# Moving the weight preparation of a fused attention and MoE kernel between VectorE and GpSimd

## The chip, the cores and the metric

The kernel runs on one core of one Trainium2 chip. The core has five queues that run side by side and wait for each other by semaphores: TensorE (PE, with its weight loads PEld), VectorE (DVE), ScalarE (ACT), GpSimd (POOL) and SyncE (SP), which here issues all transfers between the chip's main memory and the on-chip buffers. Each queue is strictly in order: an instruction that waits holds up everything behind it on its engine. The metric is the device time of one execution in microseconds (us).

## The reference

Windowed attention over 8 batches, 8 heads, 576 positions and 64 values per head, and behind it a feed-forward layer whose activation is h times softmax(h), normalized and scaled:

```python
scores = scale * np.matmul(q, k.transpose(0, 1, 3, 2))
mask = (rel >= 0) & (rel < window)            # rel = query - key, window = 64
scores = np.where(mask, scores, -1000000000.0)
attn = softmax(scores)                        # maximum taken off, sum + 1e-09
x = (attn @ v)                                # 4608 tokens x 512
h = x @ w_in                                  # 512 x 1024, float64
solu = h * softmax(h)
ln = (solu - mu) / np.sqrt(var + 1e-06) * g_ln
return (ln @ w_out).astype(np.float32)        # 1024 x 512, float64
```

The weights w_in and w_out come as 64-bit floats, which the kernel turns into 32-bit floats itself; g_ln, q, k and v are 32-bit.

## The kernel before

The 4608 tokens are 36 tiles of 128. For each tile t the kernel computes eight heads of scores on TensorE (`scores`, L376, into pS), a softmax (`softmax`), the transposes of the attention weights (`transposes`, L471, copied to PT), the product with v (`values`, L495, into pX, copied to xH and its rest xL), the first feed-forward product (`moe_in`, into pH), the activation and normalization (`moe_norm`, e and the small column buffer mst), a transpose of e, and the second product (`moe_out`, into pO), which is copied out.

A product in full precision is made of three passes with weights split into an upper part H and a rest, here called the lower half (L532, L660). Tiles 0 to 2 in `moe_in` and tile 0 in `moe_out` instead use the whole 32-bit weights in slower plain matmuls (L521, L650), because the split weights are not ready by then.

The weights are prepared during the first tiles. They are eight blocks of 128 x 1024: blocks 0 to 3 are w_in, 4 to 7 are w_out. `weight_block` takes the two 32-bit halves of each 64-bit number: absolute value of the high half (ScalarE, L290), clamp of it to the exponent range (L292), then on VectorE a mask and shift (L294) and two merges with the raw data (L296, L298); for w_out two multiplies by the gain (L302, GpSimd), one for each half of the block. `split` makes the H part (ScalarE, L316) and the lower half as W - H (VectorE, L318), in two halves x = 0 and x = 1 of 512 columns. Lower half i lies in buffer w_(8+i). The ring of w buffers holds nine, so lower half i (i over 0) reuses the buffer of weight block i - 1 and waits for the plain matmuls that read that block.

Softmax: for tile 0 each head has its own instruction on VectorE that adds the mask and takes the minimum of the negated scores (L389), its exponential (ScalarE, L403) and its scale by 1/sum (VectorE, L417). Every other tile has one instruction for all heads' scores (L394) and one for all maxima (L399), and its eight scales are on GpSimd (L417). Tiles 1 to 34 turn e by the transfer engine: `planes` separates the two 16-bit halves of e (VectorE, L592, two instructions a tile, into pl), `turn` stores them (yd) and reads them back transposed (yT). The other tiles turn e on TensorE. The masked attention windows need a joined copy of v (`join`, vx, GpSimd for the first eight tiles). GpSimd also takes the power of the variance (L565) and applies the normalization to e (L569).

The instructions of all queues are recorded as operations with an engine and an estimated cost. `Plan.order` fixes the order of each queue from these costs: it derives from TensorE's recorded order when each operation is due, and places on each engine, among the operations that are ready, the one due first. TensorE's own operations keep the order they were recorded in. A change of an operation's engine or cost so moves others on the same engine. The reads and writes of each operation and the ring sizes give the waits.

Of the kernel before, what the change touches and what calls it, by code (L numbers as in the profile page):

```python
# [36 lines left out]
JOINS = 8  # L37

# [133 lines left out]
def tile_window_attention_solu_moe(  # L172
# [96 lines left out]
    def weight_block(i, src, g):  # L269
# [21 lines left out]
        engine, eng, cost = ("DVE", nc.vector, 700) if i < 2 else ("POOL", nc.gpsimd, 1540)  # L291
        plan.op(engine, cost, lambda: eng.tensor_scalar(  # L292
# [7 lines left out]
        if g is not None:  # L300
            for x in range(2):
                plan.op("POOL", 780, lambda x=x: nc.gpsimd.tensor_scalar(  # L302
                    tf()[:, x], tf()[:, x], g(x), 0.0, ALU.mult, ALU.add), [("g",), W], [("w", i, x)])
# [9 lines left out]
    def split(i):  # L313

        for x in range(2):
            plan.op("ACT", 600, lambda x=x: nc.scalar.copy(WH(i, x), W32(i)[:, x]),  # L316
                    [("w", i), ("w", i, x), ("w", NC + 1 if i < NC else NW - 1)], [("H", i, x)])
            plan.op("DVE", 690, lambda x=x: nc.vector.tensor_sub(  # L318
                WL(i)[:, x], W32(i)[:, x], WH(i, x).bitcast(F32)),
                [("w", i), ("w", i, x), ("H", i, x)], [("w", NW + i, x)])  # L320
# [24 lines left out]
    def join(t):  # L345

        b = t if first_of(t) == 0 else t - 1
        engine, copy, cost = ("POOL", nc.gpsimd.tensor_copy, 780) if t < JOINS else ("ACT", nc.scalar.copy, 590)
        plan.op(engine, cost, lambda: copy(VX(t)[:WIN], V(t)[:WIN]), [("v", t)], [("vx", t, 0)])
        plan.op(engine, cost, lambda: copy(VX(t)[WIN:], V(b)[WIN:]), [("v", b)], [("vx", t, 1)])  # L350

    def SS(t):
        return T("sS", t, [P, H, P])
# [28 lines left out]
    def softmax(t):  # L382
        def cols(tag, h):
            return T(tag, t, [P, H], pool=st)[:, h:h + 1]

        mk = masks[first_of(t)]
        if t == 0:
# [14 lines left out]
        for h in range(H):  # L402
            plan.op("ACT", 580, lambda h=h: nc.scalar.activation(  # L403
                SS(t)[:, h], SS(t)[:, h], AF.Exp, bias=cols("nmx", h), scale=1.0 if t else -1.0,
                accum_out=cols("sm", h)),
                [("nmx", t, h)], [("sS", t, h), ("sm", t, h)], lat=200)
# [8 lines left out]
        engine, v, cost = ("POOL", nc.gpsimd, 400) if t else ("DVE", nc.vector, 150)  # L415
# [170 lines left out]
    def planes(t):  # L586
        if not crosses(t):
            return
        for h in range(2):
            hs = slice(h * 512, (h + 1) * 512)  # L590
            engine, eng, cost = ("DVE", nc.vector, 700)
# [195 lines left out]
```

## Time and profile before

| | us |
|---|---|
| median of 3 runs (lowest to highest) | 562.27 (562.09 to 562.64) |
| profiled execution | 562.74 |
| its span, first to last instruction | 561.0 |
| busy in the span: TensorE | 522.4 (93%) |
| VectorE | 392.4 (70%) |
| ScalarE | 329.9 (59%) |
| GpSimd | 307.8 (55%) |

Busy time is an average over stages. The views used below are the 40 slices of the page (each digit is a tenth of busy time or of full TensorE clock), stretches of time with each engine's busy time, groups of instructions by line and shape, the timeline of one engine, and the chain of work that ended last: followed back from the last instruction, at each step to what released it. In a timeline row the bracket gives the idle time before the instruction and what ended it.

### The profile page before, as it was taken

How to read it: one execution, taken by the hardware profiler on the slowest of the kernel's cores; microseconds unless marked ns; L12 is line 12 of the kernel's file. 1: busy time of each engine (PE TensorE's matmuls, PEld its weight loads, DVE VectorE, ACT ScalarE, POOL GpSimd, SP SyncE). 2: the span in 40 equal slices, each digit the busy share in tenths (PEclk: the TensorE clock that was granted, in tenths of full speed). 3: DMA queues.
4: the chain of work that ended last, by engine and by line, in shares of the span. 5: the costliest groups of instructions: out<-in, count | busy, mean ns of one | idle time of the engine just before them, and what ended most of it. 6: DMA issues, size and time to landing. Idle time of an engine off the chain costs nothing.

```text
span 561.0 us, 11235 instructions
## 1 busy us (share of the span) xinstructions
PE 522.4 (93%) x4088; PEld 401.9 (72%) x4088; DVE 392.4 (70%) x707; ACT 329.9 (59%) x955; POOL 307.8 (55%) x495
## 2 busy tenths in 40 slices
PE   1678679899999999999999999999999999999997
PEld 1334347678788887777777777777777777777865
DVE  4974787767778786868686868676777777755330
ACT  4357565657666666666666666666666677643431
POOL 3839993746556465555555554646464648652110
PEclk9975788999999999999999999999999999999999
DMA  8970211583998999898988998999998995876210
GB/s 350 404 268 20 65 67 43 178 221 123 278 245 234 259 235 236 235 255 221 253 250 238 237 263 235 238 258 232 260 247 227 262 222 177 217 184 164 61 39 37
DMA packets 153079, 115.56 MB, mean 206 GB/s; under 512 B 129856, under 2 KB 129856, under 8 KB 152512
## 3 DMA queue, kind: packets, MB, share of 16 engines
q1 hardware_dynamic: 153024, 114.84, 74.5%
q8 instruction: 32, 0.52, 0.4%
q14 instruction: 23, 0.19, 0.1%
HBM read 41.42 MB, written 41.42 MB: 148 GB/s over the span
## 4 chain that ended last, share of the span: by engine, by line
PE 81%; POOL 6%; DVE 6%; DMA 3%; issue 2%; ACT 0%; SPq 0%; POOLq 0%; ACTq 0%
PE pO L660 36%; PE pH L532 33%; PE pX L495 6%; PE pS L376 6%; POOL sS L417 3%; DMA raw<-w_in 2%; DMA g_sb<-gT 2%; POOL w L292 2%; DVE w L298 1%; DVE sS L394 1%; DVE w L296 1%; DVE mst L547 1%; POOL w L302 1%; DVE w L318 1%; PE t L471 1%
## 5 line engine op out<-in xcount | busy, mean ns | idle before, releaser
L417 POOL TENSOR_SCALAR sS<-sS,rec 128x128 f32<-128x128 f32 x280 | 120.4, 452 | 125.4 <-DVE mst L556 61.8
L403 ACT ACTIVATE sS<-sS,nmx 128x128 f32<-128x128 f32 x288 | 112.0, 392 | 47.1 <-DVE nmx L399 39.9
L660 PE MATMUL pO<-w_outH,yH 128*128 128x512 f32 x280 | 114.7, 410 | 1.6 <-ACT ot L667 1.0
L660 PE MATMUL pO<-w,yH 128*128 128x512 f32 x280 | 110.9, 396 | 0.0
L660 PE MATMUL pO<-w_outH,yL 128*128 128x512 f32 x280 | 110.2, 394 | 0.0
L532 PE MATMUL pH<-w_inH,xH 128*128 128x512 f32 x264 | 106.8, 405 | 1.5 <-DVE mst L552 1.5
L532 PE MATMUL pH<-w,xH 128*128 128x512 f32 x264 | 105.0, 402 | 0.0
L532 PE MATMUL pH<-w_inH,xL 128*128 128x512 f32 x264 | 104.6, 396 | 0.0
L628 DVE TENSOR_TENSOR yL<-yT,yH 128x512 fp32r<-128x512 f32 x66 | 72.0, 1094 | 41.8 <-ACT yH L626 41.7
L569 POOL TENSOR_SCALAR e<-e,mst 128x512 f32<-128x512 f32 x72 | 64.8, 907 | 40.6 <-DVE mst L566 33.3
L626 ACT CAST yH<-yT 128x512 fp32r<-128x512 f32 x66 | 41.0, 622 | 56.6 <-issue 43.8
L547 DVE TENSOR_REDUCE mst<-pH 128x1 f32<-128x1024 f32 x36 | 44.0, 1223 | 38.6 <-PE pH L532 38.3
L660 PEld LDWEIGHTS pO<-w_outH,yH 128*128 128x128 f32 x280 | 52.5, 187 | 19.0 <-issue 4.8
L660 PEld LDWEIGHTS pO<-w_outH,yL 128*128 128x128 f32 x280 | 52.6, 188 | 13.8 <-DVE yL L640 0.9
L532 PEld LDWEIGHTS pH<-w_inH,xH 128*128 128x128 f32 x264 | 50.0, 189 | 14.7 <-ACT w_outH L316 1.6
L660 PEld LDWEIGHTS pO<-w,yH 128*128 128x128 f32 x280 | 52.6, 188 | 10.8
L532 PEld LDWEIGHTS pH<-w_inH,xL 128*128 128x128 f32 x264 | 50.2, 190 | 12.7 <-DVE xL L506 0.3
L532 PEld LDWEIGHTS pH<-w,xH 128*128 128x128 f32 x264 | 50.2, 190 | 11.6 <-issue 0.2
L437 POOL COPY raw<-sS 128x1024 uint16<-128x1024 uint16 x56 | 57.1, 1049 | 0.0
L403 ACT ACTIVATION_READ_ACCUMULATOR sS<-sS,nmx 128x1 f32 x288 | 54.6, 190 | 0.0
L505 ACT CAST xH<-pX 128x512 fp32r<-128x512 f32 x33 | 19.4, 586 | 57.7 <-PE pX L495 57.6
L376 PE MATMUL pS<-qk 64*64 64x128 f32 x1152 | 42.4, 288 | 9.4 <-DMA qk<-qk 7.2
(81 smaller groups left out, 810.4 us busy)
## 6 DMA issues: line engine op xcount, KB each, us to landing
qk<-qk SPq DMA_DIRECT2D x36, 640.0 KB, 4.9
yd<-pl SPq DMA_DIRECT2D x33, 512.0 KB, 3.4
pd<-raw SPq DMA_DIRECT2D x28, 512.0 KB, 3.3
v<-vS SPq DMA_DIRECT2D x36, 256.0 KB, 3.5
y<-ot SPq DMA_DIRECT2D x36, 256.0 KB, 2.6
raw<-w_in SPq DMA_DIRECT2D x4, 1024.0 KB, 9.0
raw<-w_out SPq DMA_DIRECT2D x4, 1024.0 KB, 8.4
yT<-yd SPq DMA_TRANSPOSE x33, 4.9
```

The source lines that it names most:

```text
L376: nc.tensor.matmul(PS(t)[half * WIN:(half + 1) * WIN, r, p], q[rs, p, half * WIN:(half + 1) * WIN], keys, start=True, stop=True)
L403: plan.op("ACT", 580, lambda h=h: nc.scalar.activation(SS(t)[:, h], SS(t)[:, h], AF.Exp, bias=cols("nmx", h), scale=1.0 if t else -1.0, ac ...
L417: plan.op(engine, cost, lambda h=h: v.tensor_scalar(SS(t)[:, h], SS(t)[:, h], rec()[:, h:h + 1], 0.0, ALU.mult, ALU.add), [("rec", t)], [( ...
L437: plan.op(engine, cost, lambda x=x, copy=copy: copy(PP(t)[:, :, 4 * x:4 * x + 4].rearrange("p k h n -> p k (h n)"), SS(t)[:, 4 * x:4 * x + ...
L495: nc.tensor.matmul(PX(t)[r * D:(r + 1) * D, p, ks], (V if half else VX)(t)[:, h * D:(h + 1) * D], PT(t)[:, r * NPAIR + p, ks], start=True, ...
L505: plan.op("ACT", 560, lambda: nc.scalar.copy(XH(t), PX(t)), [("pX", t)], [("xH", t)])
L532: plan.op("PE", 233, lambda n=n, c=c, x=x, w=w: nc.tensor.matmul(PH(t)[:, hs], x(t)[:, c], WH(c, h) if w is WH else WL(c)[:, h], start=(n ...
L547: plan.op("DVE", 1230, lambda: nc.vector.tensor_reduce(nmax(), PH(t), axis=AX.X, op=ALU.max, negate=True), [("pH", t)], [key(0)])
L569: plan.op("POOL", 770, lambda h=h, hs=hs: nc.gpsimd.tensor_scalar(E(t)[:, hs], E(t)[:, hs], nmean(), kk(), ALU.add, ALU.mult), [key(4), ke ...
L626: plan.op("ACT", 560, lambda hs=hs: nc.scalar.copy(YH(t)[:, hs], YT(t)[:, hs]), [("yT", t)], [("yH", t, h)])
L628: plan.op("DVE", 690, lambda hs=hs: nc.vector.tensor_sub(YL(t)[:, hs], YT(t)[:, hs], YH(t)[:, hs].bitcast(F32)), [("yT", t), ("yH", t, h)] ...
L660: plan.op("PE", 233, lambda f=f, i=i, x=x, k=k, y=y, w=w: nc.tensor.matmul(PO(), y(t)[:, f], w(i, x), start=(f == k == 0), stop=(f == NF - ...
```

## The change

Six edits, all in the first tiles' work:

- The clamps of weight blocks 2 to 7 go from GpSimd to VectorE, which had those of blocks 0 and 1.
- The x = 1 half of each lower half goes from VectorE to GpSimd, eight subtractions.
- The planes of the tiles below 4 go from VectorE to GpSimd. Tile 0 has none, so these are tiles 1, 2 and 3.
- Tiles 1 and 2 get their scores and maxima head by head, as tile 0 had.
- The scales of tiles 1 and 2 go from GpSimd to VectorE.
- The estimated costs of some GpSimd operations, and of VectorE's scale, are changed, which only acts on the order.

```diff
+PLANES = 4
+HEADS = 3
+SCALES = 3
...
-        engine, eng, cost = ("DVE", nc.vector, 700) if i < 2 else ("POOL", nc.gpsimd, 1540)
-        plan.op(engine, cost, lambda: eng.tensor_scalar(
+        plan.op("DVE", 700, lambda: nc.vector.tensor_scalar(
             tf(), tf(), EXP_LO, EXP_HI, ALU.max, ALU.min), [W], [W])
...
-                plan.op("POOL", 780, lambda x=x: nc.gpsimd.tensor_scalar(
+                plan.op("POOL", 860, lambda x=x: nc.gpsimd.tensor_scalar(
                     tf()[:, x], tf()[:, x], g(x), 0.0, ALU.mult, ALU.add), [("g",), W], [("w", i, x)])
...
-            plan.op("DVE", 690, lambda x=x: nc.vector.tensor_sub(
+            engine, eng, cost = (("DVE", nc.vector, 690), ("POOL", nc.gpsimd, 1000))[x]
+            plan.op(engine, cost, lambda x=x, eng=eng: eng.tensor_sub(
                 WL(i)[:, x], W32(i)[:, x], WH(i, x).bitcast(F32)),
...
-        engine, copy, cost = ("POOL", nc.gpsimd.tensor_copy, 780) if t < JOINS else ("ACT", nc.scalar.copy, 590)
+        engine, copy, cost = ("POOL", nc.gpsimd.tensor_copy, 860) if t < JOINS else ("ACT", nc.scalar.copy, 590)
...
-        if t == 0:
+        if t < HEADS:
             for h in range(H):
                 plan.op("DVE", 370, lambda h=h: nc.vector.tensor_tensor_reduce(
...
-                SS(t)[:, h], SS(t)[:, h], AF.Exp, bias=cols("nmx", h), scale=1.0 if t else -1.0,
+                SS(t)[:, h], SS(t)[:, h], AF.Exp, bias=cols("nmx", h), scale=-1.0 if t < HEADS else 1.0,
...
-        engine, v, cost = ("POOL", nc.gpsimd, 400) if t else ("DVE", nc.vector, 150)
+        engine, v, cost = ("POOL", nc.gpsimd, 400) if t >= SCALES else ("DVE", nc.vector, 170)
...
-            engine, eng, cost = ("DVE", nc.vector, 700)
+            engine, eng, cost = ("POOL", nc.gpsimd, 1050) if t < PLANES else ("DVE", nc.vector, 700)
             plan.op(engine, cost, lambda h=h, hs=hs, eng=eng: eng.tensor_copy(
                 PL(t)[:, :, hs], E(t)[:, hs].bitcast(U16).rearrange("p (n k) -> p k n", k=2)),
```

Lines behind these edits move by four or five in the changed kernel (L292 becomes L296, L417 becomes L422). TensorE's queue is the same, instruction by instruction. On the other queues the order moves at three places that the prediction speaks of. A name is the buffer's tag, the tile or weight block, and a running number.

VectorE, from the clamp of weight block 1 to the last merge of block 3. Before:

```order
L292 TENSOR_SCALAR w_1_214<-w_1_214 128x1024
L294 TENSOR_SCALAR w_1_214<-w_1_214 128x1024
L296 SCALAR_TENSOR_TENSOR w_1_214<-raw_1_147,w_1_214 128x1024
L294 TENSOR_SCALAR w_2_224<-w_2_224 128x1024
L298 SCALAR_TENSOR_TENSOR w_1_214<-raw_1_147,w_1_214 128x1024
L296 SCALAR_TENSOR_TENSOR w_2_224<-raw_2_149,w_2_224 128x1024
L294 TENSOR_SCALAR w_3_246<-w_3_246 128x1024
L298 SCALAR_TENSOR_TENSOR w_2_224<-raw_2_149,w_2_224 128x1024
L296 SCALAR_TENSOR_TENSOR w_3_246<-raw_3_153,w_3_246 128x1024
L394 SCALAR_TENSOR_TENSOR sS_1_310<-pS_1_252,maskNone_99 128x1024
L298 SCALAR_TENSOR_TENSOR w_3_246<-raw_3_153,w_3_246 128x1024
```

Now, the same stretch:

```order
L296 TENSOR_SCALAR w_1_214<-w_1_214 128x1024
L296 TENSOR_SCALAR w_2_222<-w_2_222 128x1024
L298 TENSOR_SCALAR w_1_214<-w_1_214 128x1024
L298 TENSOR_SCALAR w_2_222<-w_2_222 128x1024
L300 SCALAR_TENSOR_TENSOR w_1_214<-raw_1_147,w_1_214 128x1024
L296 TENSOR_SCALAR w_3_245<-w_3_245 128x1024
L300 SCALAR_TENSOR_TENSOR w_2_222<-raw_2_149,w_2_222 128x1024
L298 TENSOR_SCALAR w_3_245<-w_3_245 128x1024
L302 SCALAR_TENSOR_TENSOR w_1_214<-raw_1_147,w_1_214 128x1024
L300 SCALAR_TENSOR_TENSOR w_3_245<-raw_3_153,w_3_245 128x1024
L302 SCALAR_TENSOR_TENSOR w_2_222<-raw_2_149,w_2_222 128x1024
L302 SCALAR_TENSOR_TENSOR w_3_245<-raw_3_153,w_3_245 128x1024
```

Two clamps have come in, and tile 1's scores stand behind block 3.

GpSimd, from tile 2's join on. Before:

```order
L349 COPY vx_2_293<-v_2_161 64x512
L292 TENSOR_SCALAR w_4_318<-w_4_318 128x1024
L417 TENSOR_SCALAR sS_1_310<-sS_1_310,rec_1_384 128x128 x8
L302 TENSOR_SCALAR w_4_318<-w_4_318,g_sb_110 128x512
L417 TENSOR_SCALAR sS_2_342<-sS_2_342,rec_2_423 128x128 x8
L292 TENSOR_SCALAR w_5_416<-w_5_416 128x1024
L349 COPY vx_3_472<-v_3_163 64x512
L350 COPY vx_3_472<-v_2_161 64x512
L302 TENSOR_SCALAR w_4_318<-w_4_318,g_sb_110 128x512
L292 TENSOR_SCALAR w_6_476<-w_6_476 128x1024
L417 TENSOR_SCALAR sS_3_387<-sS_3_387,rec_3_485 128x128 x8
L292 TENSOR_SCALAR w_7_483<-w_7_483 128x1024
```

Now, the same engine from tile 3's scales on:

```order
L422 TENSOR_SCALAR sS_3_417<-sS_3_417,rec_3_497 128x128 x8
L323 TENSOR_TENSOR w_8_541<-w_0_165,w_inH_108 128x512
L306 TENSOR_SCALAR w_4_317<-w_4_317,g_sb_110 128x512
L354 COPY vx_4_584<-v_4_294 64x512
L355 COPY vx_4_584<-v_3_163 64x512
L306 TENSOR_SCALAR w_4_317<-w_4_317,g_sb_110 128x512
L323 TENSOR_TENSOR w_9_612<-w_1_214,w_inH_108 128x512
L323 TENSOR_TENSOR w_10_620<-w_2_222,w_inH_108 128x512
L422 TENSOR_SCALAR sS_4_548<-sS_4_548,rec_4_618 128x128 x8
L323 TENSOR_TENSOR w_11_673<-w_3_245,w_inH_108 128x512
L306 TENSOR_SCALAR w_6_459<-w_6_459,g_sb_110 128x512 x2
```

The clamps and the scales of tiles 1 and 2 are gone (between tile 2's join and tile 3's scales only tile 3's join and block 5's two multiplies are left), and the subtractions stand among the scales, w_9 to w_11 of which wait for tile 2's plain matmuls.

VectorE at tile 1's scales. Now:

```order
L419 RECIPROCAL rec_1_370<-rec_1_370 128x8
L394 ISA sS_2_353,nmx_2_354<-pS_2_332,maskNone_99 128x128
L394 ISA nmx_2_354 128x1
L422 TENSOR_SCALAR sS_1_311<-sS_1_311,rec_1_370 128x128 x3
L552 TENSOR_REDUCE mst_0_398<-pH_0_297 128x1
L422 TENSOR_SCALAR sS_1_311<-sS_1_311,rec_1_370 128x128 x5
L399 SCALAR_TENSOR_TENSOR sS_3_417<-pS_3_381,maskNone_99 128x1024
L300 SCALAR_TENSOR_TENSOR w_4_317<-raw_4_209,w_4_317 128x1024
L557 ISA e_0_414,mst_0_398<-pH_0_297,e_0_414 128x1024
```

ScalarE, at tile 2's copies, before and now:

```order
L476 COPY PT_2_517<-t_8_504 128x512
L476 COPY PT_2_517<-t_9_511 128x512
L316 CAST w_inH_108<-w_1_214 128x512
L549 ACTIVATE e_1_564,mst_1_519<-pH_1_463,mst_1_519 128x1024
L503 COPY xH_2_571<-pX_2_545 128x512
```

```order
L481 COPY PT_2_538<-t_8_505 128x512
L554 ACTIVATE e_1_543,mst_1_511<-pH_1_462,mst_1_511 128x1024
L481 COPY PT_2_538<-t_9_514 128x512
L320 CAST w_inH_108<-w_1_214 128x512
L320 CAST w_inH_108<-w_2_222 128x512 x2
L508 COPY xH_2_582<-pX_2_557 128x512
```

Five of tile 1's scales stand behind the maximum of pH_0 on VectorE, and on ScalarE tile 1's exponential has moved ahead of tile 2's second copy, three splits now standing ahead of xH_2.

## The prediction

> **What bounds the kernel now.** I read first the page's 40 slices (14 us each), then the engines' busy time by stretch, then the chain of work that ended last.
>
> ```profile
> PE   1678679899999999999999999999999999999997
> PEclk9975788999999999999999999999999999999999
> ```
>
> TensorE fills up only in the eighth slice, and its granted clock dips to half in the fourth. By stretch (us; busy us and instructions of PE, PEld, DVE, ACT, POOL; clock; DMA share; GB/s):
>
> ```profile
> 0.00:114.00 114.00, 80.59 (x649) 50.18 (x649) 84.49 (x143) 61.39 (x174) 80.35 (x108) 0.85 0.50 176
> 38.00:66.00 28.00, 18.92 (x142) 10.45 (x132) 17.38 (x26) 18.96 (x49) 25.51 (x31) 0.73 0.22 66
> 66.00:92.00 26.00, 22.47 (x124) 14.70 (x125) 20.62 (x37) 13.74 (x44) 19.93 (x24) 0.77 0.11 36
> 114.00:500.00 386.00, 386.00 (x3150) 308.43 (x3148) 286.11 (x518) 250.44 (x749) 216.37 (x377) 1.00 0.90 234
> ```
>
> From 114 to 500 TensorE has no gap and a full clock. The change leaves its queue in the same order, so nothing done there by other engines can be worth anything; the gain or loss is how much earlier or later TensorE enters that stretch, with tile 1's first output matmul (pO_1). What sets that moment is in the chain in order of time (start, us, what):
>
> ```profile
> 29.58 2.08 PE pH L521 x2
> ...
> 40.69 3.51 POOL sS L417 x7
> ...
> 44.88 2.83 POOL sS L417 x8
> 47.71 3.59 POOL w L292
> ...
> 59.04 4.81 POOL sS L417 x8
> ...
> 72.12 1.65 DVE w L296
> ...
> 82.23 5.58 PE pH L532 x12
> ...
> 114.01 5.81 PE pO L660 x24
> ```
>
> From 40.7 to 72.1 the chain lies on GpSimd almost without a break, and the row of 38 to 66 has GpSimd busy 25.5 of 28 us: weight clamps (L292), attention scales (L417), gain multiplies. From 72 to 114 it is mostly VectorE. So the start-up is bound by GpSimd, then by VectorE, and TensorE waits.
>
> **The change, part by part.** Durations by group (busy us, mean ns of one; the idle time before follows). All but the copies of L437 and the reduction L547, which are of the whole run, are of the first 116 us:
>
> ```profile
> L292 POOL TENSOR_SCALAR w<-w 128x1024 f32<-128x1024 f32 x6 | 23.2, 3863 | 1.8 <-ACT w L290 1.8
> L292 DVE TENSOR_SCALAR w<-w 128x1024 f32<-128x1024 f32 x2 | 1.4, 688 | 6.7 <-ACT w L290 6.7
> L417 POOL TENSOR_SCALAR sS<-sS,rec 128x128 f32<-128x128 f32 x48 | 22.6, 494 | 13.4 <-DVE rec L414 10.6 <-DVE mst L561 2.8
> L389 DVE CUSTOM_DVE_ANT_0 sS<-pS,mask 128x128 f32<-128x128 f32 x8 | 1.8, 288 | 0.0
> L394 DVE SCALAR_TENSOR_TENSOR sS<-pS,maskNone 128x1024 f32<-128x1024 f32 x7 | 8.5, 1215 | 3.1 <-PE pS L376 3.0
> L318 DVE TENSOR_TENSOR w<-w,w_inH 128x512 fp32r<-128x512 f32 x8 | 6.5, 822 | 0.0
> L592 DVE COPY pl<-e 128x1024 uint16<-128x1024 uint16 x4 | 3.1, 793 | 1.2 <-POOL e L569 1.2
> L437 POOL COPY raw<-sS 128x1024 uint16<-128x1024 uint16 x56 | 57.1, 1049 | 0.0
> L547 DVE TENSOR_REDUCE mst<-pH 128x1 f32<-128x1024 f32 x36 | 44.0, 1223 | 38.6 <-PE pH L532 38.3
> ```
>
> Off GpSimd: six clamps, 23.2 us, and the scales of tiles 1 and 2, 16 x 0.494 = 7.9. Onto it: eight lower halves L318 and the planes of tiles 1 to 3 (tile 0 is turned on TensorE, so "four" is three), six copies. The planes have the shape of L437: 6 x 1.05 = 6.3 us. A two-input 128x512 subtraction on GpSimd is not in the trace. Below, it cannot beat VectorE's 0.82; above, the 128x1024 clamp at 3.86 gives 1.93 for half the columns. I take 1.25, nearer the lower end, because the clamp applies two limits to each element: 8 x 1.25 = 10. GpSimd before 114 goes from 80.4 to 80.4 - 23.2 - 7.9 + 10 + 6.3 = 65.6 us.
>
> The Trainium skill, "GPSIMD Engine Reference", section 4.1 Engine selection, advises against this half of the change: two-input elementwise work belongs on VectorE, being about twice as slow on GpSimd. Its 4497 ns for 2048 columns would make an estimated 1.12 us per subtraction and 9 us for eight. No run here shows it, and the total on GpSimd moves by 1 us.
>
> VectorE gains six clamps (4.1 us) and 16 scales, loses eight subtractions (6.6) and six copies (4.8), and in two tiles trades L394 and an equally long maximum (2.4) for eight heads at 0.29 (2.3). Nothing shows a scale alone on VectorE: tile 0's eight took 2.95 us beside GpSimd's copies (below), 0.37 each; from below 0.21, the step between heads of L389. At 0.3 they cost 4.8. VectorE goes from 84.5 to about 82 us: it does not get lighter, it stops waiting.
>
> **Step 1, tile 0's last weight.** VectorE's timeline (start, us, line, shapes, idle before):
>
> ```profile
> 13.73 2.95 DVE L417 TENSOR_SCALAR sS<-sS,rec 128x128 f32<-128x128 f32 x8
> 16.60 0.68 DVE L292 TENSOR_SCALAR w<-w 128x1024 f32<-128x1024 f32 x1
> 28.15 1.37 DVE L298 SCALAR_TENSOR_TENSOR w<-raw,w 128x1024 int32<-128x1024 int32 x1
> ```
>
> Between 16.60 and 29.52 stand ten weight operations, stretched by GpSimd's clamps, and tile 1's scores. Now twelve weight operations stand there alone: six of 0.69 and six of 1.22 make 11.5; begun 0.8 earlier, since the scales of tile 0 no longer run beside a clamp, they end at 27.3, 2.2 sooner. The matmul on it (2.08), tile 2's scores (1.96 in the chain) and the second half follow:
>
> ```profile
> 33.50 3.81 PE L521 MATMUL pH<-w,xH 128*128 128x512 f32 x8
> 40.77 2.23 PE L471 MATMUL t<-ident,sS 128*128 128x128 f32 x6 [2.43 <-POOL sS L417]
> 44.80 0.59 ACT L476 COPY PT<-t 128x512 f32<-128x512 f32 x1 [0.85 <-PE t L471]
> 48.09 10.17 PE L521 MATMUL pH<-w,xH 128*128 128x512 f32 x16 [0.68 <-ACT xH L503]
> 66.69 9.39 PE L521 MATMUL pH<-w,xH 128*128 128x512 f32 x16 [5.44 <-DVE mst L552]
> ```
>
> Tile 0's moe_in ends at 27.3 + 2.1 + 2.0 + 3.8 = 35.2.
>
> **Step 2, tile 1.** The heads of tile 1 and their exponentials (eight of 0.39 with a 0.19 read) are ready before that, so this edit costs and brings nothing here; without that cover it would show its 2.3 us. Five of tile 1's eight scales are queued on VectorE behind the maximum of pH_0, and tile 1's transposes wait for them: 35.2 + 1.2 + 5 x 0.3 = 37.9. Last transposes 0.5, copy 0.6, then the 2.7 that lay between the end of that copy (45.39) and 48.09: moe_in(1) starts at 41.7, 6.4 earlier. VectorE's next queue, up to the maximum of pH_1, is eight operations of 1.2, two of 0.69 and eight scales, some 13 us less what is done, ending near 50; moe_in(1) ends at 41.7 + 10.2 = 51.9, so it is covered.
>
> **Step 3, tile 2.** The new ScalarE order puts tile 1's exponential between the two copies of tile 2's transposes; the second copy so waits for the maximum of pH_1. With the exponential of
>
> ```profile
> L549 ACT ACTIVATE e<-pH,mst 128x1024 f32<-128x1024 f32 x5 | 5.6, 1115 | 4.7 <-DVE mst L547 4.0 <-DVE rec L411 0.7
> ```
>
> and its read (0.19): 51.9 + 1.2 + 1.3 + 0.6 + 2.7 = 57.7 for moe_in(2), 9.0 earlier. The 5.44 us before it, VectorE held by clamped weights, shrink to two gaps of about 1.
>
> **Step 4, tile 3.** moe_in(2) takes 9.4: 67.1. VectorE then does maximum 1.2, tile 3's copy 0.7, one lower half 0.7, tile 5's scores 1.2, the product with e 1.2: moe_in(3) at 72.1, 10.1 before 82.23. Its second halves read GpSimd's subtractions of weights 0 to 3; the fourth ends near 71.5, eight matmuls ahead.
>
> **Step 5, tile 1's output.** From moe_in(3) to pO_1 TensorE runs as before, save the wait for tile 7's scores:
>
> ```profile
> 112.91 1.10 PE L376 MATMUL pS<-qk 64*64 64x128 f32 x32 [2.22 <-DVE sS L394]
> ```
>
> VectorE's queue ahead of those scores loses four lower halves and two copies: I take 1 us off. That is 11.1 earlier at the old clock. Two of the shortened gaps no longer hold TensorE idle; if the clock stays up in half of the two cases, moe_in(2) at the rate of 33.50 (7.6 for 9.4) and the first half of moe_in(3) (2.8 for 5.6) are worth 4.6, half of it 2.3. Sum: 11.1 + 2.3 = 13.4, call it 13.
>
> The cover of this is GpSimd's chain to yT_1, the turned tile 1:
>
> ```profile
> 80.49 3.57 POOL L417 TENSOR_SCALAR sS<-sS,rec 128x128 f32<-128x128 f32 x8 [0.82 <-DVE rec L414]
> 89.95 0.92 POOL L565 TENSOR_TENSOR mst<-mst,neghalf 128x1 f32<-128x1 f32 x1 [4.67 <-DVE mst L556]
> 91.25 1.52 POOL L569 TENSOR_SCALAR e<-e,mst 128x512 f32<-128x512 f32 x2 [0.38 <-ACT sS L403]
> 95.35 0.35 SPq L599 DMA_DIRECT2D yd<-pl  x1
> 106.05 1.13 ACT L626 CAST yH<-yT 128x512 fp32r<-128x512 f32 x2
> ```
>
> From 59.04 (tile 3's scales) to 92.77 GpSimd spent 33.7 us, 5.9 of them idle and 3.9 on a clamp. Now it starts near 50 (weight 5's last operation on VectorE and its two gain multiplies come first), has 23.9 of that work, five subtractions (6.3), two gain multiplies (1.4), two planes (2.1), and a wait of some 4.5 for moe_in(2)'s fifth matmul, behind which tile 4's scales, tile 0's normalization and tile 1's planes are queued: near 88. From the store to the split took 10.7: 99. pO_1 needs it at 114 - 13 = 101. Cover 2 us: each microsecond that a subtraction takes beyond 1.25 delays four of them behind that wait, 4 us, and 2 of these show.
>
> **Against the runs.** The profiled execution took 562.74 us, 561.0 of it span. 562.74 - 13 = 549.7; the median of the three runs is 0.47 lower. I forecast 549.3.
>
> **Rivals.**
>
> *Clock stays full.* The clock was 0.50 in
>
> ```profile
> 42.00:48.00 6.00, 4.19 (x37) 2.80 (x36) 2.15 (x8) 3.92 (x11) 6.00 (x14) 0.50 0.01 4
> ```
>
> after a gap of 2.43. If gaps near 1 us no longer cost it, moe_in(1) saves 2.6 and the other half of step 5 2.3: 13 + 4.9 = 18, 544.3. VectorE allows it: 82 us of work from 6.7 end at 89 without any idle time, and pO_1 would come at 96. Against: between 36 and 41.7 TensorE still idles for about 3 us.
> The Trainium skill, "TensorE: Matmul & The Clock Gate", Part 1, has the clock fall after an idle window of about 3.4 us and gives the rule of no longer gaps; that rule is this rival. The trace disagrees where a 2.43 gap was enough.
>
> *GpSimd's new work comes late.* Subtractions at 1.93 use the cover up and 0.7 more; with scales and multiplies stretched as at 59.04 (4.81 for 2.83), yT_1 comes 4 to 5 late: gain about 8, 554.3. For it: VectorE's two-input work runs throughout beside them. Against: eight of L318's stand on VectorE no longer.
>
> *VectorE is the bound.* Its 82 us are in order, with waits for pH_0, moe_in(2) and tile 4's transposes inside; from 6.7 on, 25 us of idle time instead of about 12 would return everything: 562.
>
> *Slower.* One mechanism: GpSimd's subtraction ahead of yT_1. With 4 of them behind moe_in(2) the forecast's 13 and the cover 2 are used up at 1.25 + 15/4 = 5 us each, more than the whole 128x1024 clamp; at 6 us, pO_1 comes 4 late, 566. Nothing in the rows is that slow.
>
> **Chances.** Forecast (gain 10.5 to 15.5) 0.62; full clock 0.13; late GpSimd 0.17; VectorE the bound 0.04; slower 0.04. Within 0.2% (1.1 us) is about what a measurement cannot tell from no change. Faster 0.92, same 0.04, slower 0.04. Range: from the full clock, 543.5, to the late GpSimd and a little over, 555.5; left out are the last two rivals and the far tail of each side.
>
> **What would show it.** Right: no gap of TensorE over 3 us after 31; moe_in(1), (2), (3) starting near 41.7, 57.7, 72.1; pO_1 near 101; the 386 us behind it unchanged; no long GpSimd stretch in the chain before 66. Wrong: TensorE waiting for yH_1 or yL_1 ahead of pO_1 (late GpSimd); a subtraction over 2 us; VectorE idle before tile 1's scales; gaps behind pO_1, where I assume none.

## The result and the profile after

The changed kernel takes 548.0 us (547.2 to 548.7), against 562.2 us (562.1 to 562.6) before on the same chip: 0.9746 of it, 95% interval 0.9729 to 0.9763. On another chip, beside the experiments below, the same kernel took 547.15 against 563.38: 0.9719 (0.9704 to 0.9733). The profiled execution of the change took 548.0 us, 546.2 of it span; the span before was 561.0. The forecast was 549.3, its range 543.5 to 555.5.

The 40 slices of the page after, of 13.7 us each, and its chain of work that ended last, summed by engine:

```profile
PE   1688799899999999999999999999999999999997
PEclk9999889999999999999999999999999999999999
PE 87%; DVE 8%; issue 2%; ACT 2%; DMA 1%; ACTq 0%
```

The slice at half clock is gone (the fourth; now two at eight tenths), and so is GpSimd's share of the chain. By stretch after (us; busy us and instructions of PE, PEld, DVE, ACT, POOL; clock; DMA share; GB/s):

```profile
38.00:66.00 28.00, 21.84 (x160) 11.78 (x156) 27.95 (x45) 19.88 (x55) 19.72 (x25) 0.94 0.22 68
100.00:486.00 386.00, 386.00 (x3148) 308.42 (x3147) 284.40 (x516) 251.04 (x751) 217.68 (x380) 1.00 0.92 235
```

From 38 to 66 GpSimd had been busy 25.51 of 28 us; now VectorE is, with 27.95. From 100 on TensorE has no gap for 386 us, as before from 114 on. So the whole difference is made ahead of pO_1. TensorE's timeline after, with the places of the prediction's steps (the instructions in between are left out):

```profile
29.94 3.70 PE L526 MATMUL pH<-w,xH 128*128 128x512 f32 x8
...
39.43 7.10 PE L526 MATMUL pH<-w,xH 128*128 128x512 f32 x16 [1.13 <-DVE mst L557]
...
52.29 8.83 PE L526 MATMUL pH<-w,xH 128*128 128x512 f32 x16 [0.90 <-ACT xH L508]
...
69.26 0.77 PE L537 MATMUL pH<-w_inH,xH 128*128 128x512 f32 x1 [1.81 <-ACT w_outH L320]
...
98.08 1.10 PE L381 MATMUL pS<-qk 64*64 64x128 f32 x32 [1.66 <-DVE sS L399]
99.12 0.50 PE L665 MATMUL pO<-w_outH,yH 128*128 128x512 f32 x1
```

moe_in(1) starts 8.7 us earlier than before (48.09), moe_in(2) 14.4 (66.69), moe_in(3) 13.0 (82.23), pO_1 14.8 (113.94), and 14.8 us is what the span lost.

A correction of names: the scores at 98.08 are those of tile 8. Ahead of pO_1 the program computes the scores of two tiles in one pass of its loop, 7 and 8, and the row is the ninth group of scores on TensorE. The prediction and the expectations call them tile 7's, and the read by VectorE that they wait for tile 6's; it is the read of tile 7's. Times and waits are not touched by this.

### The profile page after: what moved, and what is told of

It is laid out like the page before. It is cut to its first block, busy times and chain, and to the rows that moved or that the text cites. A ratio compares the mean times of both kernels' runs of the same rounds, so it can differ in the third digit from the quotient of the medians.

```text
span 546.2 us, 11264 instructions
## 1 busy us (share of the span) xinstructions
PE 514.9 (94%) x4088; PEld 397.8 (73%) x4088; DVE 391.0 (72%) x743; ACT 329.2 (60%) x955; POOL 296.4 (54%) x487
## 4 chain that ended last, share of the span: by engine, by line
PE 87%; DVE 8%; issue 2%; ACT 2%; DMA 1%; ACTq 0%
PE pO L665 37%; PE pH L537 34%; PE pX L500 6%; PE pS L381 6%; DVE w L300 1%; PE pH L526 1%; PE pO L655 1%; DVE w L296 1%; DMA raw<-w_in 1%; DVE w L302 1%; DVE sS L422 1%; DVE mst L552 1%; DVE sS L399 1%; ACT sS L408 1%; PE t L476 1%
## 5 line engine op out<-in xcount | busy, mean ns | idle before, releaser
L422 POOL TENSOR_SCALAR sS<-sS,rec 128x128 f32<-128x128 f32 x264 | 111.4, 441 | 112.4 <-DVE mst L561 61.9
L574 POOL TENSOR_SCALAR e<-e,mst 128x512 f32<-128x512 f32 x72 | 60.7, 849 | 40.1 <-DVE mst L571 32.1
```

The lines of the kernel that those rows point to most:

```text
L422: plan.op(engine, cost, lambda h=h: v.tensor_scalar(SS(t)[:, h], SS(t)[:, h], rec()[:, h:h + 1], 0.0, ALU.mult, ALU.add), [("rec", t)], [( ...
L574: plan.op("POOL", 770, lambda h=h, hs=hs: nc.gpsimd.tensor_scalar(E(t)[:, hs], E(t)[:, hs], nmean(), kk(), ALU.add, ALU.mult), [key(4), ke ...
```

## The experiments

Each is the changed kernel with one edit, unless said otherwise. Ratios are against the kernel before on the same chip; the changed kernel's own is 0.9719 to 0.9746. So 0.001 of a ratio is 0.56 us.

**The changed kernel once more.**

> The changed kernel itself, unchanged, so that edits of a few tenths of a per cent are compared with it on one chip. Every theory expects the ratio of the first measurement, 0.9746.

Measured 0.9719 (0.9704 to 0.9733), 547.15 us. Its profiled span is 545.3, 0.9 less than that of the first. The difference is in the first half of moe_in(0): four matmuls take 2.26 us in one execution and 3.68 in the other, behind the same wait of 1.15 us. So single executions of this kernel differ by about a microsecond through the clock alone, and edits are judged by the medians.

**The clamps alone, in the kernel before.**

```diff
-        engine, eng, cost = ("DVE", nc.vector, 700) if i < 2 else ("POOL", nc.gpsimd, 1540)
-        plan.op(engine, cost, lambda: eng.tensor_scalar(
+        plan.op("DVE", 700, lambda: nc.vector.tensor_scalar(
```

> The kernel before, with the six clamps of weight blocks 2 to 7 on VectorE and nothing else changed. Clamp theory: they are most of the gain, because the chain of the kernel before lay on GpSimd from 40.7 to 72.1 and the clamps are 23.2 us of its 80.4 before 114. VectorE goes from 84.5 to 84.5 + 4.1 = 88.6 us, which still fits in front of an earlier pO_1, but its queue becomes the tighter one. I expect 11 of the 14 us: 551. Sum theory (the rival): the clamps alone only move the bound from GpSimd to VectorE, which also keeps all the lower halves and planes, and half the gain comes from the other edits: 555 or more.

Measured 552.99 against 563.05, 0.9822 (0.9806 to 0.9839): 10.1 us, about two thirds of the change's 14 to 16. The clamp theory holds. What it leaves on the way, in TensorE's timeline:

```profile
36.78 1.18 PE L470 MATMUL t<-ident,sS 128*128 128x128 f32 x3 [3.37 <-POOL sS L416]
...
44.94 9.81 PE L520 MATMUL pH<-w,xH 128*128 128x512 f32 x16 [0.68 <-ACT xH L502]
```

Tile 1's transposes still wait for its scales on GpSimd, and moe_in(1) starts 5.5 us later than in the change and runs at half clock until about 50.

**The clamps back on GpSimd.**

```diff
-        plan.op("DVE", 700, lambda: nc.vector.tensor_scalar(
+        engine, eng, cost = ("DVE", nc.vector, 700) if i < 2 else ("POOL", nc.gpsimd, 1540)
+        plan.op(engine, cost, lambda: eng.tensor_scalar(
```

> The changed kernel, with the clamps of blocks 2 to 7 back on GpSimd. GpSimd gets 23.2 us back less nothing, 75.8 + 23.2 = 99 us ahead of a pO_1 that now comes at 99.1. Clamp theory: GpSimd is again what bounds the start, with more work than in the kernel before (80.4), so the time is that of the kernel before or up to 6 us over it: 562 to 568. Rival: the other edits have a worth of their own (VectorE has 82 us less 4.1 for clamps), and the time lies between: 555.

Measured 557.09, 0.9890 (0.9875 to 0.9904). My theory that GpSimd would bound everything again falls: 6.0 us of the gain stay without the clamps. Clamps alone 10.1, all the rest alone 6.0, together 14.2 (first chip) to 16.2 (second): the two add up to the second figure, and to 1.9 us more than the first. The rest is not incidental, and the next four runs say which part of it works.

**The heads back.**

```diff
-HEADS = 3
+HEADS = 1
```

> The changed kernel, with the scores of tiles 1 and 2 in one instruction each and all maxima in another, as in the kernel before. Prediction's theory: the heads cost and bring nothing, since they and their exponentials are done before the scales can run: within 0.1% of the changed kernel. Order theory (the rival): the exponentials of a tile can start 2.1 us earlier with heads, and because of that the order places tile 1's scales directly around the maximum of pH_0; without them the scales stand behind the product with e_0 and a weight merge, some 4 us later than 35.8, and moe_in(1) with them. VectorE does its weights in that time instead, so 2 to 3 us of it show at pO_1: 0.4 to 0.5% above the changed kernel.

Measured 553.33, 0.9827 (0.9811 to 0.9842): 6.2 us slower than the changed kernel beside it. The prediction's theory, that this edit costs and brings nothing, falls; the order theory has the mechanism, and its size was too small by half. VectorE's timeline of this kernel, then TensorE's:

```profile
36.10 1.17 DVE L557 CUSTOM_DVE_ANT_0 e<-pH,e 128x1024 f32<-128x1024 f32 x1
...
37.20 1.65 DVE L422 TENSOR_SCALAR sS<-sS,rec 128x128 f32<-128x128 f32 x8
```

```profile
37.53 1.88 PE L476 MATMUL t<-ident,sS 128*128 128x128 f32 x8 [4.07 <-DVE sS L422]
...
58.53 8.96 PE L526 MATMUL pH<-w,xH 128*128 128x512 f32 x16 [5.74 <-ACT sS L408]
```

There is no idle time in front of these VectorE rows: the scales are not late because the exponentials are late (tile 1's end near 32), but because the order puts them behind the product with e_0. In the change the last five of them start at 34.82. TensorE gets a gap of 4.07 us, and moe_in(1) starts 3.2 us later than in the change (42.67 for 39.43).

The second gap, 5.74 us, has another cause. Tile 2's scales are not late (41.43 for 41.30). The row names ScalarE's exponentials, but moe_in(2) does not read them, and its xH_2 was done at 55.2. What it waits for is that VectorE's product with e_1 has read pH_1, and that ends at 58.37, in the same queue without idle time:

```profile
52.27 1.21 DVE L552 TENSOR_REDUCE mst<-pH 128x1 f32<-128x1024 f32 x1
...
57.16 1.21 DVE L557 CUSTOM_DVE_ANT_0 e<-pH,e 128x1024 f32<-128x1024 f32 x1
```

moe_in(1) had ended at 49.8; weight operations stand ahead of the maximum, and scores, a clamp and a tile's maxima between it and the product. In the change this product ends 4.8 us behind moe_in(1), here 8.6. So moe_in(2) starts at 58.53 instead of 52.29, 6.2 us later. The edit's worth is the place that the order gives to tile 1's scales, and to the maximum and the product of pH_1, in VectorE's queue.

**The planes back on VectorE.**

```diff
-PLANES = 4
+PLANES = 0
```

> The changed kernel, with the planes of tiles 1 to 3 on VectorE again. Tail theory: what is left before pO_1 is VectorE's queue ahead of tile 7's scores, and two tiles' planes (4 x 0.79 = 3.2 us) stand in it again, tile 2's of them directly behind its normalization: pO_1 comes 1.5 to 3 us later, a ratio 0.3 to 0.5% above that of the changed kernel beside it. Neutral theory (the rival): VectorE is idle for 5 us between 66 and 92, and GpSimd loses 6.3 us, so nothing shows: the ratio of the changed kernel within 0.1%.

Measured 550.05, 0.9764 (0.9751 to 0.9777): 2.9 us slower than the changed kernel beside it, at the upper end of the tail theory. VectorE's queue in front of its read of tile 7's scores:

```profile
92.25 0.75 DVE L597 COPY pl<-e 128x1024 uint16<-128x1024 uint16 x1 [0.68 <-POOL e L574]
...
93.52 1.77 DVE L597 COPY pl<-e 128x1024 uint16<-128x1024 uint16 x1
...
95.28 1.28 DVE L633 TENSOR_TENSOR yL<-yT,yH 128x512 fp32r<-128x512 f32 x2
...
98.59 1.21 DVE L399 SCALAR_TENSOR_TENSOR sS<-pS,maskNone 128x1024 f32<-128x1024 f32 x1
```

Tile 2's planes stand ahead of the read of tile 7's scores, which frees the score buffer for tile 8 at 99.8; TensorE's gap there grows from 1.66 to 2.81 us.

**The lower halves back on VectorE.**

```diff
-            engine, eng, cost = (("DVE", nc.vector, 690), ("POOL", nc.gpsimd, 1000))[x]
+            engine, eng, cost = ("DVE", nc.vector, 690)
```

> The changed kernel, with all lower halves on VectorE again. VectorE theory: VectorE is busy 27.95 of 28 us from 38 to 66 and sets when moe_in(3) starts, so four more lower halves of 0.68 ahead of it show nearly whole, 2.7 us: 550.7. GpSimd theory (the rival): GpSimd's subtractions of 1.26 to 1.81 us stretch VectorE's work beside them and delay yT_1, so taking them off is worth as much as it costs: 548, or 547.

Measured 547.91, 0.9730 (0.9715 to 0.9744), not to be told from the changed kernel. But it gets there differently. TensorE's timeline:

```profile
64.80 0.77 PE L537 MATMUL pH<-w_inH,xH 128*128 128x512 f32 x1 [1.42 <-DVE mst L557]
...
96.99 1.19 PE L381 MATMUL pS<-qk 64*64 64x128 f32 x32 [2.40 <-DVE sS L399]
...
98.70 0.63 PE L665 MATMUL pO<-w,yH 128*128 128x512 f32 x1
```

moe_in(3) starts 4.5 us earlier than in the change (0.7 of it is there at moe_in(2) already), although VectorE has more to do. In VectorE's timeline the maximum of pH_2, behind which the order now puts a merge that stood ahead of it, starts at 60.37 instead of 64.00:

```profile
59.76 0.69 DVE L323 TENSOR_TENSOR w<-w,w_inH 128x512 fp32r<-128x512 f32 x1
60.37 1.22 DVE L552 TENSOR_REDUCE mst<-pH 128x1 f32<-128x1024 f32 x1
```

Then the lead is given back. Tile 5's transposes, at 87.61, have to wait for its scales on GpSimd, the gap ahead of tile 8's scores is 2.40 instead of 1.66, and the clock falls behind it, so that the first seven matmuls of pO_1 take about 0.63 instead of 0.40. So a lead at moe_in(3) is worth little; what counts is when VectorE is through with tile 7's scores. This part of the change brings nothing.

**The scales of tiles 1 and 2 back on GpSimd.**

```diff
-SCALES = 3
+SCALES = 1
```

> The changed kernel, with the scales of tiles 1 and 2 on GpSimd again. GpSimd stood idle for 10.12 us from 28 to 38 and 6.68 us from 39.6 to 46.2, which is where these scales would run (eight in 3.3 to 4.8 us by the rows of tile 3). VectorE theory: VectorE loses 2 x 1.65 = 3.3 us in its full stretch and the scales hide in GpSimd's idle time: 545.5 to 546.5, faster than the change. Chain theory (the rival, what the change seems meant for): the scales stand directly in front of the transposes of tiles 1 and 2, so each tile waits 3.3 to 4.8 instead of 1.65 us on its way: 550 to 551.

Measured 547.45, 0.9720 (0.9706 to 0.9735): no difference either. Both theories fall. VectorE's queue loses 3.3 us, but the sixteen scales take 3.79 and 7.92 us on GpSimd beside VectorE's weights, and the gap ahead of moe_in(2) is 2.24 us instead of 0.90. So what VectorE saves seems to be lost there; the two were not separated.

Taken out one at a time, the clamps are worth some 10 us, the heads 6.2 and the planes 2.9, which is 19 against 16.2 for the whole change on that chip: the parts overlap. The halves and the scales are worth nothing that the measurements show. The sixth edit, the estimated costs, was not run alone.

**Gaps filled.** The new function fill(n) puts n plain matmuls of the identity with itself into TensorE's queue.

```diff
+            if t + 1 in FILL_X:
+                fill(FILL_X[t + 1])
             on(values, t + 1)
...
+        if t in FILL_IN:
+            fill(FILL_IN[t])
         on(moe_in, t, 0)
```

> The changed kernel, with 48 plain 128x128 matmuls on the identity added to TensorE's queue: 11 before tile 2's products with v, 6 before moe_in(2), 18 before tile 3's products with v, 13 before moe_in(3), about as long as the gaps there (1.54, 0.90, 2.58 and 1.81 us). All other queues keep their order; what the added matmuls compute is never read. Clock theory: it is these gaps that take the clock down, so moe_in(2) takes 7.1 instead of 8.83 us and the first half of moe_in(3) 2.8 instead of 4.89; VectorE is not free before 63.9 for the maximum of pH_2, so only the second shows, 2.1 us and 0.6 for the values: 545.5, 0.4 to 0.5% less. Give-back theory (the rival): moe_in(3) ends 2 us earlier, but tile 7's scores wait for VectorE until the same time: within 0.15% of the changed kernel, with a longer gap ahead of tile 7's scores.

Measured 548.59 (546.99 to 548.66), 0.9732 (0.9716 to 0.9748): no gain. By stretch (columns as above), and the last gap in TensorE's timeline:

```profile
38.00:66.00 28.00, 27.44 (x222) 18.73 (x223) 28.00 (x46) 19.61 (x55) 21.03 (x27) 1.00 0.21 68
66.00:92.00 26.00, 26.00 (x207) 19.60 (x204) 20.66 (x40) 17.64 (x54) 24.05 (x33) 1.00 0.32 97
```

```profile
97.10 1.70 PE L384 MATMUL pS<-qk 64*64 64x128 f32 x32 [2.03 <-DVE sS L402]
```

The clock is full from 38 to 92, as the clock theory wants, and moe_in(2) takes 7.03 us instead of 8.83. But the fillers took twice what I had planned for them (2.72 us for the first eleven): moe_in(2) starts 1.2 us and moe_in(3) 1.5 us later than in the changed kernel on that chip, and at tile 7's scores only 0.4 us of lead is left (93.97 for 94.37). This is given back, as the give-back theory has it: tile 8's scores start at 97.10, where they start at 97.13. In one execution of four the clock stayed full to the end, and its span is 545.2; those of the changed kernel are 545.3 to 546.7. What a full clock would be worth without the fillers' own delay is not shown. VectorE's 28.00 busy us of 28 and the run with the halves back, where 4.5 us at moe_in(3) became 1.1 at tile 8's scores, speak against much.

**The subtractions twice.** Each of GpSimd's eight is issued two times in a row, the order of all queues being the same.

```diff
+            def emit(x=x, eng=eng):
+                for _ in range(1 + x):
+                    eng.tensor_sub(WL(i)[:, x], W32(i)[:, x], WH(i, x).bitcast(F32))
```

> The changed kernel, with each of GpSimd's eight subtractions issued twice in a row (the second writes the same numbers again), all queues in the same order otherwise. It prices the cover of GpSimd's chain. Prediction's theory: four subtractions stand behind moe_in(2)'s fifth matmul ahead of tile 1's planes, cover 2 us; four more of 1.26 to 1.81 us make 6 us, so pO_1 comes 4 us later: 0.7% above the changed kernel. Wider-cover theory (the rival, from the profile after): tile 1's planes end at 81.25, not 88, and the lower half of tile 1's turned activations is only read behind the matmul at 99; five more subtractions (7.5 us) less the idle time around them (1.1) put the planes at 87.6 and the split near 98.5, within 1 us of its use: no more than 0.1% above the changed kernel.

Measured 556.68, 0.9886 (0.9873 to 0.9898): 9.4 us slower by the ratio's distance to 0.9719. Both theories fall, and by far. In VectorE's timeline I saw three waits of 2.59, 1.57 and 1.39 us that end with GpSimd's subtractions (the row of the third names TensorE, but it ends with GpSimd's pair at 97.65): the lower half of block i on VectorE overwrites weight block i - 1, which GpSimd's subtraction of that block reads. The first of them:

```profile
62.87 0.69 DVE L326 TENSOR_TENSOR w<-w,w_inH 128x512 fp32r<-128x512 f32 x1 [2.59 <-POOL w L326]
```

The next experiment takes these waits away.

**The same with eleven weight buffers.**

```diff
-    "raw": 4, "w": 9, "qk": 3,
+    "raw": 4, "w": 11, "qk": 3,
...
-    plan = Plan(RINGS)
+    plan = Plan({**RINGS, "w": 9})
```

> The kernel with each of GpSimd's subtractions issued twice (9 us slower than the changed kernel), with 11 instead of 9 buffers behind the weights and the same order of every queue. With nine buffers the lower half of block i on VectorE overwrites weight block i - 1, which GpSimd's subtraction of block i - 1 reads, so VectorE's queue stands still until GpSimd is done; with eleven it overwrites block i - 3. Zigzag theory: VectorE's waits of 2.59, 1.57 and 1.39 us behind GpSimd's subtractions go, and with them most of the 9 us: 549 to 551, a ratio of 0.975 to 0.979. Late-planes theory (the rival): GpSimd's queue itself is what is late, with tile 1's planes at 86.9 instead of 81.3 and tile 5's scales at 91.1 instead of 85.5, and the time stays: 555 to 557, a ratio of 0.986 to 0.989.

Measured 555.37, 0.9861 (0.9845 to 0.9878). Those waits are gone and the time is nearly the same, so they were not the cause; GpSimd's queue itself is late. GpSimd's timeline of this kernel, then VectorE's (in it, L326 are the subtractions, L426 the scales, L574 and L575 what is L570 and L571 in the change):

```profile
88.38 2.98 POOL L326 TENSOR_TENSOR w<-w,w_outH 128x512 fp32r<-128x512 f32 x2
91.35 2.81 POOL L426 TENSOR_SCALAR sS<-sS,rec 128x128 f32<-128x128 f32 x8
94.13 0.54 POOL L574 TENSOR_TENSOR mst<-mst,neghalf 128x1 f32<-128x1 f32 x1
```

```profile
94.71 1.25 DVE L575 TENSOR_TENSOR mst<-mst 128x1 f32<-128x1 f32 x1 [4.18 <-POOL mst L574]
...
98.58 1.17 DVE L637 TENSOR_TENSOR yL<-yT,yH 128x512 fp32r<-128x512 f32 x1
...
102.09 1.21 DVE L403 SCALAR_TENSOR_TENSOR sS<-pS,maskNone 128x1024 f32<-128x1024 f32 x1
```

TensorE's timeline shows what waits for it, tile 8's scores and then pO_1:

```profile
103.36 1.99 PE L385 MATMUL pS<-qk 64*64 64x128 f32 x32 [3.93 <-DVE sS L403]
105.28 0.79 PE L669 MATMUL pO<-w_outH,yH 128*128 128x512 f32 x1
105.87 0.63 PE L669 MATMUL pO<-w,yH 128*128 128x512 f32 x1
```

The changed kernel has the same queue, with GpSimd's power at 88.73 and this wait on VectorE:

```profile
88.73 0.55 POOL L570 TENSOR_TENSOR mst<-mst,neghalf 128x1 f32<-128x1 f32 x1
```

```profile
89.31 1.24 DVE L571 TENSOR_TENSOR mst<-mst 128x1 f32<-128x1 f32 x1 [1.51 <-POOL mst L570]
...
96.82 1.21 DVE L399 SCALAR_TENSOR_TENSOR sS<-pS,maskNone 128x1024 f32<-128x1024 f32 x1
```

The power of a tile's normalization stands on GpSimd behind tile 5's scales and all subtractions recorded ahead of them. VectorE's one-element product waits for it at the head of its queue, and behind that stand yL_1 and the read of tile 7's scores. The power comes 5.4 us later and the read of tile 7's scores 5.3. With the clock down behind the longer gap, tile 8's scores take 0.9 us more and the first nine matmuls of pO_1 (0.63 for 0.40) 1.7: 7.9 us, as between the two spans (554.1 and 546.2).

**Tile 8's scores behind pO_1.**

```diff
-            for a in ahead(t):
+            for a in ahead(t)[:1]:
                 on(scores, a)
...
             on(moe_out, t - BEHIND)
+            for a in ahead(t)[1:]:
+                on(scores, a)
```

> The changed kernel, with tile 7's scores placed behind pO_1's matmuls in TensorE's order instead of in front of them. The last gap ahead of the dense stretch is the 1.66 us in which these scores wait for VectorE to read tile 6's. Last-wait theory: the gap closes and nothing else changes: 1.66 us, 0.3% below the changed kernel. Rival: pO_1 itself needs tile 1's lower half yL_1, which VectorE computes in the same queue just before tile 6's scores, so TensorE waits there instead and the ratio is that of the changed kernel within 0.1%.

Measured 546.57, 0.9707 (0.9694 to 0.9719). The gap is gone: tile 7's scores at 95.48 are followed by pO_1 at 96.52. The span of the profiled execution, 544.8, is under the two of the changed kernel (546.2 and 545.3), and the median is the lowest of all kernels here, but the interval overlaps that of the changed kernel, so a gain of its own is not shown.

**Both: halves back and late scores.**

```diff
-            engine, eng, cost = (("DVE", nc.vector, 690), ("POOL", nc.gpsimd, 1000))[x]
+            engine, eng, cost = ("DVE", nc.vector, 690)
...
-            for a in ahead(t):
+            for a in ahead(t)[:1]:
                 on(scores, a)
...
+            for a in ahead(t)[1:]:
+                on(scores, a)
```

> The changed kernel, with all lower halves on VectorE again and tile 7's scores behind pO_1. With the halves back moe_in(3) started 4.5 us sooner (64.80 against 69.26) and yet pO_1 only 1.0 sooner and then 1.6 us at half clock, which the 2.40 us ahead of tile 7's scores explains. Last-wait theory: without that gap the gain of the earlier moe_in(3) is kept: 2.4 + 1.6 = 4 us under the kernel with the halves back, 0.7% below the changed kernel and better than both. Rival: tile 1's turned activations are split at 90.9 to 95.8 by VectorE and ScalarE whatever TensorE does, so pO_1 waits for them at 95 to 96 and half of it is lost again: 0.3 to 0.4% below.

Measured 548.39 (543.86 to 548.67), 0.9725 (0.9701 to 0.9749). No gain, except in one execution of six, whose span is 542.1. GpSimd takes the place of the wait removed, in TensorE's timeline:

```profile
86.41 0.33 PE L476 MATMUL t<-ident,sS 128*128 128x128 f32 x1 [0.77 <-POOL sS L422]
...
89.39 1.88 PE L476 MATMUL t<-ident,sS 128*128 128x128 f32 x5 [1.01 <-POOL sS L422]
```

GpSimd's timeline of the same kernel:

```profile
85.24 5.50 POOL L422 TENSOR_SCALAR sS<-sS,rec 128x128 f32<-128x128 f32 x8 [4.71 <-DVE rec L419]
```

moe_in(3) starts at 65.06, but the transposes of tile 5 wait four times for its scales, and GpSimd begins these only at 85.24, since it waits for VectorE's reciprocal. That is late because of one lower half ahead of it on VectorE:

```profile
75.48 4.57 DVE L323 TENSOR_TENSOR w<-w,w_outH 128x512 fp32r<-128x512 f32 x1
```

The same subtraction takes 0.68 us in the kernel with the halves back. Here GpSimd's copy, normalization and planes run beside it, from 75.44 to 79.51. So VectorE lost 3.9 us to GpSimd ahead of tile 5's scales, and what the two edits are worth together without that loss is not shown. Whether the execution of 542.1 is one without it is not known, since it has no trace.

## Why the prediction was right, and where it was not

**What bounds, and where the gain is read.** Right: nothing changed behind pO_1 (386.00 of 386 us before and after), GpSimd left the chain, and the gain is the 14.8 us by which pO_1 came earlier. Forecast were 13 for the profiled execution.

**The prices of the operations.** Groups after, up to 114 us:

```profile
L323 POOL TENSOR_TENSOR w<-w,w_inH 128x512 fp32r<-128x512 f32 x4 | 6.1, 1532 | 1.1 <-DVE rec L416 0.7 <-ACT pl L563 0.4
L323 POOL TENSOR_TENSOR w<-w,w_outH 128x512 fp32r<-128x512 f32 x4 | 5.6, 1391 | 0.9 <-ACT w_outH L320 0.9
L597 POOL COPY pl<-e 128x1024 uint16<-128x1024 uint16 x6 | 6.0, 1037 | 0.0
L422 DVE TENSOR_SCALAR sS<-sS,rec 128x128 f32<-128x128 f32 x24 | 5.6, 299 | 0.0
```

The subtraction costs 1.53 and 1.39 us, within its bounds of 0.82 and 1.93 and 0.14 to 0.28 above the 1.25 taken: 11.7 us for eight, not 10. The Trainium skill's figure ("GPSIMD Engine Reference", section 3.1 Elementwise — side-by-side cycle accounting) had given an estimate of 1.12, which the shortest here (1.26) come near and the longest (1.81) do not. That page's advice against this half of the change (section 4.1 Engine selection) is borne out by the run with the halves back: moving them brought nothing. The planes are as taken (1.04 for 1.05). The scales of tiles 1 and 2 on VectorE were taken too dear: sixteen of them occupied it for 0.68 + 1.06 + 1.65 = 3.4 us, not 4.8, since one begins before the last has ended, and the mean of 0.30 in the row counts that overlap twice.

**Steps 1 and 2.** moe_in(0) ended at 33.64 (forecast 35.2), moe_in(1) started at 39.43 (41.7) and took 7.10 us (10.2). The mis-sized term is the clock. I kept the old clock for both and gave the clock gain only 2.3 us in all; here the scores between moe_in(0)'s halves took 1.10 instead of 2.0, and moe_in(1) saved 3.1 by itself. VectorE's last merge of block 3 was also 0.9 earlier than forecast (26.38 for 27.3). The last wait ahead of moe_in(1) is not the one of the step: it is VectorE's product with e_0, to 39.28, while xH_1, where the step's path ends, was done at 39.02.

**Step 3.** From the end of moe_in(1) to the start of moe_in(2) I had 5.8 us; it was 46.53 to 52.29, 5.8. The path is right, the exact figure is partly luck: VectorE was not free at the end of moe_in(1), as step 2 has it, and took the maximum 0.8 later (47.31), and the way from the last copy to moe_in(2) took 2.1 instead of 2.7.

**Step 4.** Failed in one term: VectorE free at the end of moe_in(2). The queue that the step lists (maximum, copy, lower half, scores, product) is as it is in VectorE's timeline, and takes 5.1 us (5.0 forecast):

```profile
61.90 2.18 DVE L302 SCALAR_TENSOR_TENSOR w<-raw,w 128x1024 int32<-128x1024 int32 x1
64.00 1.21 DVE L552 TENSOR_REDUCE mst<-pH 128x1 f32<-128x1024 f32 x1
...
67.89 1.21 DVE L557 CUSTOM_DVE_ANT_0 e<-pH,e 128x1024 f32<-128x1024 f32 x1
```

But moe_in(2) ended at 61.1 and the maximum began at 64.00: a merge of 2.18 us (1.22 without GpSimd's subtraction beside it) was still in front. So of the 6.0 us that the end of moe_in(2) was ahead of the forecast, 2.9 were given back here. (TensorE's row of moe_in(3) names a split of w_out on ScalarE as what ended its wait. moe_in(3) does not read that; the product above, which ends at 69.10, frees the buffer that it writes.)

**Step 5.** pO_1 came at 99.12 (near 101). The wait ahead of tile 8's scores went from 2.22 to 1.66, not to 1.2. The cover was looked for at the wrong place. Tile 1's planes were done at 81.25, not near 88, and the way by yT_1 had room. What has almost no cover is GpSimd's power, through VectorE's product to the read of tile 7's scores. In the change VectorE waits 1.51 us for it, and the only slack behind is 0.32 us of waiting for tile 5's transposes. Doubled subtractions cost 9 us, where the step's rule gives 4 x 1.5 less 2, some 4. The chain before shows GpSimd at this place, where I had read "mostly VectorE" (start, us, what):

```profile
98.53 4.71 POOL sS L417 x8
103.24 0.52 POOL mst L565
104.14 2.88 POOL e L569 x2
```

**The total.** moe_in(2) started 5.4 us ahead of the forecast, moe_in(3) 2.8 and pO_1 1.9. That the forecast time is within 1.3 us of the measured one is so in part luck: a clock gain that I had put too low, and a VectorE that was less ready than I had assumed, offset each other.

**The heads.** "Costs and brings nothing here" was wrong by 6.2 us. I priced the instructions and their readiness, and did not ask what the order would do without them. The forecast did not suffer, since steps 2 and 3 started from the new order as it is.

**The rivals.** Full clock: the clock did rise, to 0.94 from 38 to 66, and 544.3 was not reached; with the gaps filled a full clock brought no gain either, though the fillers' own delay leaves open what it would bring without them. Late GpSimd: not in the change, though it begins at once when a subtraction grows. VectorE the bound: true as a statement on the stretch from 38 to 66 and on the end at tile 7's scores, but with 14.8 us gained by then. Slower: no subtraction was over 1.81.

## What to carry to other kernels

Where queues are strictly in order, price an edit by the place that it gives its work in the queue, not by its instructions alone: heads that cost the same on VectorE were worth 6 us, and halves that left VectorE were worth nothing. A lead in the middle of a start-up is only kept if the last wait ahead of the dense stretch moves too; find that wait first, follow each engine's queue ahead of it back to the smallest instruction that crosses engines (here a power of one element per partition), and count from there how much delay there is room for.

## What the runs showed of the hardware

**GpSimd stood still beside VectorE.** GpSimd's timeline after:

```profile
13.52 1.17 POOL L355 COPY vx<-v 64x512 f32<-64x512 f32 x2
17.62 9.23 POOL L354 COPY vx<-v 64x512 f32<-64x512 f32 x1 [2.92 <-DMA v<-vS]
```

The same copy takes 0.61 and 9.23 us. The long one ends at 26.85, within half a microsecond of the last of the weight operations that VectorE ran without a break since 15.87 (26.38); it is 9.22 to 9.26 in the ten other kernels here that have these clamps on VectorE. In the kernel before, where GpSimd's clamps run beside VectorE's weight operations and stretch them, it took 0.74. It costs nothing, since tile 1's product with v reads it ten microseconds later. The Trainium skill, "SBUF — State Buffer", section Who interferes with whom, has VectorE and GpSimd share one pair of ports under an exclusive lock: VectorE's operations with two inputs in this memory contend for it with GpSimd's reads, and its two-port modes hold it for a whole instruction, while the other fully blocks. The trace agrees with the block, and shows that it can last over many instructions of VectorE: one GpSimd copy got no turn in nine of them. It goes the other way too: the lower half of 4.57 us on VectorE in the last experiment had five GpSimd instructions beside it.

**The clock does not go by the length of the last gap.** It fell behind gaps of 2.03 us (the filled kernel: 1.70 us for tile 8's scores) and 2.40 (halves back), and stayed full behind 2.81 (planes back: 1.10 us for the same scores, and 0.39 a matmul after them) and 2.22 (the kernel before). Two executions of one kernel differ in it, as told above. The Trainium skill, "TensorE: Matmul & The Clock Gate", Part 1, has the activity counted in windows that run freely and don't begin with the kernel's work; a dependence on where a gap falls in such a window would fit both, though no run here shows the windows themselves. Its condition of a whole idle window of about 3.4 us does not hold here: these gaps are shorter.
